# Second expert's weight quarters made during attention, input quarters on VectorE, closer routing rounds, and q and k loaded into unused rows of the accumulator

## The chip, the cores and the metric

One core of one Trainium2 chip. The metric is the device time of one execution in microseconds (us), median of several. All runs used here are of the fast state or, for single looks, of state unknown; one execution of before, of 861.91 us, is marked slow, and no ratio contains it. Two more sources of spread turn out to matter in this case: the clock granted to TensorE (its records show full and half speed: up to the last matmul, 41.0 us of half speed in the first trace of before, 20.5 us in its third), and the end of an execution. From the last matmul to the end, while the last outputs are written, the 16 traces took 13.0 to 17.4 us, with no order by kernel.

## The reference, cut to what matters

```python
# attention: 4 batches x 8 heads, 768 positions of 64; scores only where 6-bit hashes agree
mask = q_bucket[:, :, :, None] == k_bucket[:, :, None, :]
attn = softmax(where(mask, scale * q @ k.T, -1e9)) @ v
x = attn.transpose(0, 2, 1, 3).reshape(3072, 512)
# routing: eight rounds over P [3072, 8]
P = exp(x @ w_gate - max)
for _ in range(8):
    P /= P.sum(1, keepdims=True) + 1e-09
    P /= P.sum(0, keepdims=True) + 1e-09
    P *= N / E
# eight experts over all positions, weighted by P
out += P[:, e:e+1] * (maximum(x @ w1[e], 0) @ w2[e])
```

## The kernel before

Attention runs in eight groups (a batch and four heads each). Group n+1 is prepared while group n is computed: load q and k, transpose on VectorE (DVE), cast on GpSimd (POOL), then 26 small transfers on one queue (SyncE's; for group 0 those of q go on ScalarE's) that bring the data into the layout for the scores. The hash bits make a detour through DRAM: `ds<-kb`, `ks<-ds`.

```python
def prepare(n):
    ...
    hashed("q"); put_bits("q"); stack("q", 1)
    if n == 0:
        fetch(1, "kq")                 # bulk load of the next group, 1.5 MB, GpSimd's queue
    elif n + 1 < len(groups):
        fetch(n + 1, "q")
    ...
    get_bits("q")                      # the last small transfers of group n
    cast_v()
    if n + 1 < len(groups):
        fetch(n + 1, "v")
    if n in (1, 3):
        load_w(0, (n + 1) // 2, pin=True)
```

After attention comes what is called the transition here: the eight routing rounds, between which TensorE (PE) does steps of the first expert for the last batches, counted at 650 ns each:

```python
def plain():
    yield from first_hidden(B - 1)     # 16 steps
    yield from first_combine(B - 2)    # 16 steps
    yield from first_combine(B - 1)    # 16 steps
    yield from first_of(1, 0)          # first product of expert 1, batch 0, alone

quarters_of_x(0); quarters_of_w(1)     # GpSimd
for it in range(ITERS):
    halves = routing(it)
    next(halves)                       # VectorE: row sums, division, column sums
    got = 0
    while got < (5500 if it == 0 else 3900):
        got += next(steps, 99999)      # TensorE
    for _ in halves: pass              # TensorE: cpt = ones x column sums; VectorE: scale
for _ in steps: pass
for b in range(1, B):
    quarters_of_x(b)                   # GpSimd
```

Experts 1 to 7 form their first product with seven products of quarter matrices instead of eight (Strassen's scheme), for which sums and differences of the quarters of the input (`xd`) and of the weights (`s`) are made beforehand, four instructions each time. In those later stages the first product of one batch is woven with the second product of the batch before.

The softmax here doesn't subtract the row's maximum and nothing guards it: scores larger than these inputs give would overflow.

Of the kernel before, what the change touches and what calls it, by code (L numbers as in the profile page):

```python
# [8 lines left out]
F32 = mybir.dt.float32  # L9
# [10 lines left out]
def kernel(  # L20
# [11 lines left out]
    nc = tc.nc  # L32
# [73 lines left out]
    acc = big.tile([P, NBLK, DD], F32)  # L106
    wpool = ctx.enter_context(tc.tile_pool(name="wpool", bufs=2))
    hpool = ctx.enter_context(tc.tile_pool(name="hpool", bufs=2))

    weights = {}  # L110

# [11 lines left out]

    hts = {}
    outv = out.rearrange("(b r j m) d -> b j m r d", b=B, r=R, j=J)

    def combine(e, b):
        if (e, 2) not in weights:
# [37 lines left out]
                yield 650  # L166

    actx = ExitStack()
    ld = actx.enter_context(tc.tile_pool(name="ld", bufs=2))
    lv = actx.enter_context(tc.tile_pool(name="lv", bufs=1))  # L170
    wk = actx.enter_context(tc.tile_pool(name="wk", bufs=2))
    scr = actx.enter_context(tc.tile_pool(name="scr", bufs=4, space=bass.MemoryType.DRAM))
# [7 lines left out]
    def fetch(n, what, eng=nc.gpsimd):  # L180
        b, g = groups[n]
        for name, src in (("k", k), ("q", q)):
            if name in what:
                t = ld.tile([P, M, D], F32, tag="nat", name=name)
                pin(eng.dma_start(out=t, in_=src[b, g * HG:(g + 1) * HG].rearrange("h (r m) d -> (h r) m d", r=R)))
                nat[name, n] = t
        if "v" in what:
            t = lv.tile([P, HG, KT * D], F32, tag="v", name="v")
            vsrc = v[b, g * HG:(g + 1) * HG].rearrange("h (r m j) d -> m r h (j d)", r=R, m=M4)
            for m in range(M4):  # L190
                pin(eng.dma_start(out=t[R * m:R * (m + 1)], in_=vsrc[m]))
            nat["v", n] = t

    def prepare(n):
# [87 lines left out]
        hashed("q")  # L282
        put_bits("q")
        stack("q", 1)
        if n == 0:
            fetch(1, "kq")
        elif n + 1 < len(groups):
            fetch(n + 1, "q")
        yield 6 + 3 * lag
        if n:  # L290
# [1 line left out]
        get_bits("q")  # L292
        cast_v()
        if n + 1 < len(groups):
            fetch(n + 1, "v")
        if n in (1, 3):
            load_w(0, (n + 1) // 2, pin=True)
        if n == 2:
# [105 lines left out]
    for u in range(len(units) + 1):  # L404
        if u < len(units):
            n, h, kt = units[u]
            b, g = groups[n]
            i = u % per
            if i == 0:
                prep = prepare(n + 1) if n + 1 < len(groups) else iter(())  # L410
                due = 0
            while due is not None and due <= i:
                due = next(prep, None)
            if u + 1 < len(units):
                pts[u + 1] = scores(*units[u + 1])
        if u > 0:
            values(*units[u - 1], pts.pop(u - 1))
        if u == len(units):
            break
        if kt == 3 and h % 2 == 0 and u > 5:  # L420
            pn, ph = (n, h - 1) if h else (n - 1, HG - 1)
            pb_, pg = groups[pn]
            turn(pb_, pg * 2 + ph // 2)
            if pg == NGRP - 1 and ph == HG - 1:
                fill = filler(pb_, pb_ < 2)
                owed = 0.0
        elif u >= 2 * per:
            owed += (total if b < 3 else total - 12 * 865) / (2 * per - 8)
            while owed > 0:
                c = next(fill, None)  # L430
                if c is None:
                    break
                owed -= c
                if c == 0:
                    break
        if u % (2 * per) == 2 * per - 1:
            for _ in fill:
                pass
# [36 lines left out]
    xdp = ctx.enter_context(tc.tile_pool(name="xdp", bufs=1))  # L475

    xd = xdp.tile([P, 3, 2, B, HT], F16)
    spool = ctx.enter_context(tc.tile_pool(name="spool", bufs=2))
    upool = ctx.enter_context(tc.tile_pool(name="upool", bufs=2))
    quarters = {}  # L480
    def quarters_of_x(b):
        v = xT[:, :, b * S:(b + 1) * S].rearrange("p (dh d) (th t) -> p dh th d t", dh=2, th=2)
        b11, b12, b21, b22 = v[:, 0, 0], v[:, 0, 1], v[:, 1, 0], v[:, 1, 1]
        t2, t3, t4 = (xd[:, i, :, b, :] for i in range(3))
        eng = nc.gpsimd
        eng.tensor_tensor(t3, b22, b12, op=Alu.subtract)
        eng.tensor_tensor(b12, b12, b11, op=Alu.subtract)
        eng.tensor_tensor(t2, b22, b12, op=Alu.subtract)
        eng.tensor_tensor(t4, b21, t2, op=Alu.subtract)
        quarters[b] = dict(b11=b11, b21=b21, b22=b22, t1=b12, t2=t2, t3=t3, t4=t4)  # L490

    def quarters_of_w(e):

        t = weights[e, 1]
        lo, hi = slice(0, F // 2), slice(F // 2, F)
        a11, a12, a21, a22 = t[:, 0:2, lo], t[:, 2:4, lo], t[:, 0:2, hi], t[:, 2:4, hi]
        s = spool.tile([P, 3, 2, F // 2], F16, tag="s1")
        nc.gpsimd.tensor_tensor(s[:, 0], a21, a22, op=Alu.add)
        nc.gpsimd.tensor_tensor(a21, a11, a21, op=Alu.subtract)
        nc.gpsimd.tensor_tensor(s[:, 1], s[:, 0], a11, op=Alu.subtract)  # L500
        nc.gpsimd.tensor_tensor(s[:, 2], a12, s[:, 1], op=Alu.subtract)
        weights[e, "q"] = dict(a11=a11, a12=a12, a22=a22, s1=s[:, 0], s2=s[:, 1], s3=a21, s4=s[:, 2])

    add = nc.vector._custom_dve

    def hidden(e, b):


        if b == 2 and e < E - 1:
            if (e + 1, 1) not in weights:  # L510
                load_w(e + 1, 1)
            quarters_of_w(e + 1)
        wq, xq = weights[e, "q"], quarters[b]
        hT = hpool.tile([P, FO, S], F16, tag="h")
        hts[e, b] = hT
        lo, hi = slice(0, HT), slice(HT, S)

        def prod(bk, f, wn, xn, first):
            for do in range(2):
                yield nc.tensor.matmul(bk, wq[wn][:, do, f * P:(f + 1) * P], xq[xn][:, do, :],  # L520
                                       start=first and do == 0, stop=do == 1, skip_group_check=True)

        def keep(bk, tag):
            t = upool.tile([P, HT], F32, tag=tag, name="u")
            nc.scalar.copy(t, bk)  # L525
            return t

        def add_relu(dst, bk, u):
            add(TENSOR_ADD_SAT, out=dst, in0=bk, in1=u, s0=3e38, s1=0.0)  # L529

        def last(f, d, u2):
            yield from prod(d, f, "a22", "t4", False)
            add_relu(hT[:, FH + f, lo], d, u2)

        late = iter(())
        for f in range(FH):
            a = hps.tile([P, HT], F32, tag="a", name="a")
            yield from prod(a, f, "a11", "b11", True)
            u1 = keep(a, "u1")
            d1 = dps.tile([P, HT], F32, tag="d", name="d1")  # L540
            yield from prod(d1, f, "a12", "b21", True)
            add_relu(hT[:, f, lo], d1, u1)
            yield None
            yield from prod(a, f, "s2", "t2", False)
            u2 = keep(a, "u2")
            d2 = d2ps.tile([P, HT], F32, tag="d", name="d2")
            yield from prod(d2, f, "s3", "t3", True)
            yield None
            yield from prod(a, f, "s1", "t1", False)
            u3 = keep(a, "u3")  # L550
            add_relu(hT[:, FH + f, hi], d2, u3)
            yield from late
            yield None
            yield from prod(a, f, "s4", "b22", False)
            nc.scalar.activation(out=hT[:, f, hi], in_=a, func=Act.Relu)  # L555
            late = last(f, d2, u2)
            if f == FH - 1:
                yield from late
                late = iter(())
            yield None  # L560
# [15 lines left out]
            else:  # L576
                pin(ins)

    def first_of(e, b):
        for ins in hidden(e, b):  # L580
            if ins is None:
                yield 650
            else:
                pin(ins)

    def plain():
        yield from first_hidden(B - 1)
        yield from first_combine(B - 2)
        yield from first_combine(B - 1)
        yield from first_of(1, 0)  # L590

    quarters_of_x(0)
    quarters_of_w(1)
    steps = plain()
    for it in range(ITERS):
        halves = routing(it)
        next(halves)
        got = 0
        while got < (5500 if it == 0 else 3900):
            got += next(steps, 99999)  # L600
        for _ in halves:
            pass
    for _ in steps:
        pass
    for b in range(1, B):
        quarters_of_x(b)
    work = [(e, b) for e in range(1, E) for b in range(B)]
    for n in range(1, len(work) + 1):
        h = hidden(*work[n]) if n < len(work) else iter(())
        c = combine(*work[n - 1])  # L610
        more = True
        while more:
            more = run(h, True)
            more = run(c, True) or more


# [28 lines left out]
```

## Time and profile before

| | before |
|---|---|
| time, median of 4 | 848.65 us (847.55 to 849.67) |
| the execution that was traced | 858.17 us, span 856.4, mean granted clock 0.969 |
| transition (first L162 matmul to the end of the first one of the second expert's combine) | 66.65 us |
| from there to the last matmul | 547.0 us |
| last matmul to the end | 16.3 us |

The prediction counts the transition to the start of that last matmul and so has 66.4 us. The second row is to be kept in mind. The trace is of an execution 9.5 us slower than the median. I saw this difference and passed over it.

How to read the views: the page's slices give the busy tenths of each engine in forty equal slices. A row of the timeline gives start, duration, engine, line, operation, output and inputs; in brackets stands the idle time before it and what ended it. A row of the waits gives total, number and longest, in us.

### The profile page before, as it was taken

The page shows a single profiled execution, that of the slowest core. Times are in us where ns is not written, and L with a number is a line of the kernel's source. Part 1 is how long each engine was busy: PE and PEld are TensorE (multiplying, and loading weights), DVE is VectorE, ACT ScalarE, POOL GpSimd, SP SyncE. Part 2 cuts the span into 40 slices and gives each one's busy share as a digit, 9 for nine tenths or more (in the row PEclk, how much of TensorE's full clock was granted, in tenths as well). Part 3 has the DMA queues.
Part 4 walks back from the last instruction along what each step waited for, and adds up shares of the span by engine and source line. Part 5 has one row for each costly group of instructions (what it writes and reads, how often), then busy time and mean ns, then how long its engine had stood idle before and what let it go on. Part 6 is the DMA issues. An engine that isn't in the chain of part 4 may idle for free.

```text
span 856.4 us, 13672 instructions
## 1 busy us (share of the span) xinstructions
PE 794.9 (93%) x5404; PEld 429.3 (50%) x5404; DVE 447.5 (52%) x773; ACT 394.9 (46%) x698; POOL 192.0 (22%) x212
## 2 busy tenths in 40 slices
PE   3699999999877899999999999999999999999992
PEld 1466656566533455555555555555555555555540
DVE  4135646554487455555555555555555555555551
ACT  0587766678622555543333333433333333333320
POOL 7555245530496000120040004000400310000000
PEclk9689999999988999999999999999999999999997
DMA  7866678520002300230023003202300230001222
GB/s 226 202 158 151 145 165 201 135 59 17 1 1 49 51 1 1 50 50 1 0 50 50 1 8 54 39 1 49 50 2 1 50 50 1 1 0 59 78 77 82
DMA packets 31927, 50.60 MB, mean 59 GB/s; under 512 B 8504, under 2 KB 21304, under 8 KB 31864
## 3 DMA queue, kind: packets, MB, share of 16 engines
q0 software_dynamic: 16880, 33.30, 19.1%
q1 hardware_dynamic: 14316, 15.95, 6.9%
q8 instruction: 42, 0.69, 0.3%
q10 hardware_dynamic: 668, 0.49, 0.2%
q14 instruction: 21, 0.17, 0.1%
HBM read 53.14 MB, written 7.08 MB: 70 GB/s over the span
## 4 chain that ended last, share of the span: by engine, by line
PE 61%; DVE 4%; issue 0%; ACT 0%; ACTq 0%
PE yp L140 32%; PE a L520 16%; PE d L520 13%; DVE hT L529 3%; ACT u L525 0%; DVE acc L146 0%; ACT hT L555 0%; ACTq L525 0%
## 5 line engine op out<-in xcount | busy, mean ns | idle before, releaser
L140 PE MATMUL yp<-t,hT 128*128 128x512 f16 x1440 | 386.3, 382 | 0.0
L525 ACT COPY u<-a 128x384 f32<-128x384 f32 x336 | 161.1, 480 | 246.3 <-PE a L520 241.3
L529 DVE CUSTOM_DVE_ANT_0 hT<-d,u 128x384 f16<-128x384 f32 x336 | 179.3, 554 | 148.8 <-PE d L520 90.2
L140 PEld LDWEIGHTS <-hT 128*128 128x128 f16 x1440 | 141.8, 99 | 125.8 <-issue 5.3
L146 DVE SCALAR_TENSOR_TENSOR acc<-yp,p,acc 128x512 f32<-128x512 f32 x168 | 125.9, 749 | 114.7 <-PE yp L140 112.2
L310 ACT ACTIVATE pt<-st 128x768 f16<-128x768 f32 x192 | 147.3, 809 | 73.0 <-PE st L307 46.5
L520 PEld LDWEIGHTS <-t 128*128 128x128 f16 x896 | 87.8, 98 | 78.7 <-issue 11.4
L307 PE MATMUL st<-qs,ks 71*128 71x384 f16 x384 | 98.3, 339 | 17.2 <-DMA qs<-ds 13.0
L520 PE MATMUL d<-xd,t 128*128 128x384 f16 x448 | 109.3, 326 | 4.1 <-DVE hT L529 0.3
L520 PE MATMUL a<-xT,s 128*128 128x384 f16 x448 | 109.3, 325 | 2.3 <-ACT u L525 2.3
L520 PEld LDWEIGHTS <-s 128*128 128x128 f16 x672 | 65.8, 98 | 87.1 <-issue 13.4
L555 ACT ACTIVATE hT<-a 128x384 f16<-128x384 f32 x112 | 55.0, 491 | 74.6 <-PE a L520 74.1
L119 POOL DMA_DIRECT2D t<-in_moe_w_dram x16 | 13.5, 846 | 327.3 <-PE d L520 307.4
L323 PEld LDWEIGHTS <-pt 128*128 128x128 f16 x1152 | 62.8, 100 | 28.5 <-issue 3.9
L323 PE MATMUL num<-va,pt 128*128 128x65 f16 x1152 | 68.6, 197 | 0.6 <-ACT pt L310 0.6
L520 PE MATMUL a<-xd,s 128*128 128x384 f16 x224 | 54.7, 326 | 0.9 <-ACT u L525 0.9
L520 PE MATMUL d<-xT,t 128*128 128x384 f16 x224 | 55.1, 328 | 0.0
L520 PE MATMUL a<-xT,t 128*128 128x384 f16 x224 | 55.1, 328 | 0.0
L307 PEld LDWEIGHTS <-ks 71*128 71x128 f16 x384 | 33.4, 100 | 38.3 <-issue 13.0
L217 POOL CAST t<-acc 128x768 f16<-128x768 f32 x32 | 26.3, 827 | 92.1 <-DVE acc L216 60.7
L368 DVE TENSOR_SCALAR hT<-hp 128x384 f16<-128x384 f32 x48 | 26.7, 555 | 28.6 <-PE hp L365 28.6
L365 PE MATMUL hp<-xT,t 128*128 128x384 f16 x192 | 39.0, 325 | 0.0
(75 smaller groups left out, 452.2 us busy)
## 6 DMA issues: line engine op xcount, KB each, us to landing
t<-in_moe_w_dram POOLq DMA_DIRECT2D x16, 1024.0 KB, 8.8
out_dram<-acc SPq DMA_DIRECT2D x24, 256.0 KB
k<-in_k_dram POOLq DMA_DIRECT2D x7, 768.0 KB, 5.7
q<-in_q_dram POOLq DMA_DIRECT2D x7, 768.0 KB, 6.3
v<-in_v_dram POOLq DMA_DIRECT2D x28, 192.0 KB, 4.3
ks<-t SPq DMA_DIRECT2D x64, 48.0 KB
qs<-t SPq DMA_DIRECT2D x56, 48.0 KB
k<-in_k_dram SPq DMA_DIRECT2D x1, 768.0 KB
```

The lines of the kernel that those rows point to most:

```text
L140: yield nc.tensor.matmul(yp, hT[:, fo, j * P:(j + 1) * P], w2[:, fo, :], start=(fo == 0), stop=(fo == FO - 1))
L146: nc.vector.scalar_tensor_tensor(out=acc[:, blk, :], in0=yp, scalar=pw_[-1][:, blk, e:e + 1], in1=acc[:, blk, :], op0=Alu.mult, op1=Alu.add)
L217: pin(nc.gpsimd.tensor_copy(t16s[name][:, c, :], trs[name][:, c, :]))
L307: pin(nc.tensor.matmul(st[:, i, 0:HT], d["k"][0:KR, h, kt * P:(kt + 1) * P], d["q"][0:KR, h, i * HT:(i + 1) * HT], start=True, stop=True))
L310: pin(nc.scalar.activation(out=pt, in_=st[:, :, 0:HT], func=Act.Exp, scale=scale))
L323: pin(nc.tensor.matmul(num[:, j * (D + 1):(j + 1) * (D + 1)], pf[:, j * P:(j + 1) * P], va[:, h, kt, :], start=(kt == 0 and j == 0), stop= ...
L365: pin(nc.tensor.matmul(hp[:, 0:HT], w1[:, do, fo * P:(fo + 1) * P], xT[:, do, b * S + t * HT:b * S + (t + 1) * HT], start=(do == 0), stop= ...
L368: pin(nc.vector.tensor_scalar(hT[:, fo, t * HT:(t + 1) * HT], hp[:, 0:HT], 0.0, None, op0=Alu.max))
L520: yield nc.tensor.matmul(bk, wq[wn][:, do, f * P:(f + 1) * P], xq[xn][:, do, :], start=first and do == 0, stop=do == 1, skip_group_check=True)
L525: nc.scalar.copy(t, bk)
L529: add(TENSOR_ADD_SAT, out=dst, in0=bk, in1=u, s0=3e38, s1=0.0)
L555: nc.scalar.activation(out=hT[:, f, hi], in_=a, func=Act.Relu)
```

## The change

Its intent: keep GpSimd, beside whose instructions VectorE's took up to 2.33 us instead of 0.36, quiet during the routing rounds, then set the rounds closer. The memory for the weight quarters comes from the q and k buffers, which now land in rows of `acc` that are not used yet. The core of the diff:

```diff
+            if n == len(groups) - 1 and i == 2:
+                quarters_of_w(1)                    # last attention group, GpSimd, pinned
...
-    ld = actx.enter_context(tc.tile_pool(name="ld", bufs=2))
-                t = ld.tile([P, M, D], F32, tag="nat", name=name)
+                x = 12 if name == "k" else 15
+                t = acc[:, x:x + 3, :].rearrange("p a d -> p (a d)").rearrange("p (m d) -> p m d", d=D)
...
-        if n == 0:
-            fetch(1, "kq")
-        elif n + 1 < len(groups):
+        if n and n + 1 < len(groups):
             fetch(n + 1, "q")
...
-            fetch(n + 1, "v")
+            fetch(n + 1, "v" if n else "kqv")
...
-        eng = nc.gpsimd                             # quarters_of_x
+        eng = nc.vector
...
-        yield from first_combine(B - 1)
-        yield from first_of(1, 0)
+        yield from woven(0)                         # both of them, interleaved
...
-        while got < (5500 if it == 0 else 3900):
+        while got < (3500 if it == 0 else 3000):
...
+        if n < B:
+            quarters_of_x(n)                        # just ahead of the batch that reads it
```

## The prediction

> **What bounds the kernel now.** I read the page's slices first, then the waits of TensorE, then the order of work on VectorE and GpSimd where the slices dip. The busy tenths of the page (forty slices of 21.4 us) say where there is anything to win:

> ```profile
> PE   3699999999877899999999999999999999999992
> ...
> POOL 7555245530496000120040004000400310000000
> PEclk9689999999988999999999999999999999999997
> ```

> TensorE (PE) is the bound from about 292 us to 840 us: its waits over that stretch come to 0.3 us in all. The end (840 to 856 us) is the last output transfer, which the change doesn't touch. So only two places can give time back: the first three slices (the start), and slices 10 to 14 (214 to 300 us), where attention ends and the routing rounds run. There GpSimd (POOL) is near full exactly where PE dips. TensorE's waits from 226 to 293 us:

> ```profile
> PE cpt L466 <- DVE cs L462: 9.9, 4, 3.8
> PE a L520 <- ACT u L525: 3.2, 11, 0.4
> ```

> The tiny matmul `cpt`, one of each routing round, waits 9.9 us for VectorE (DVE). The timeline of VectorE shows why one round takes so long while GpSimd works and so little when it doesn't. The start is in the first column, the duration in the second:

> ```profile
> 238.72 1.89 DVE L460 TENSOR_TENSOR p<-p,rs 128x192 f32<-128x192 f32 x1
> ...
> 261.98 0.18 DVE L457 TENSOR_SCALAR rs<-rs 128x24 f32<-128x24 f32 x1
> 262.19 0.30 DVE L458 RECIPROCAL rs<-rs 128x24 f32<-128x24 f32 x1
> 262.52 0.36 DVE L460 TENSOR_TENSOR p<-p,rs 128x192 f32<-128x192 f32 x1
> ...
> 265.22 2.33 DVE L471 SCALAR_TENSOR_TENSOR p<-p,cr 128x192 f32<-128x192 f32 x1
> ...
> 267.97 1.59 DVE L457 TENSOR_SCALAR rs<-rs 128x24 f32<-128x24 f32 x1
> ```

> The same L460 takes 1.89 us at 238 us, with GpSimd busy, and 0.36 us at 262 us, in the four microseconds in which GpSimd waits for a weight transfer. Per round VectorE needs 2.65 us from `cpt` (L468) to the end of L462 when it is alone (0.17 + 0.20 + 0.36 + 0.35 + 0.18 + 0.30 + 0.36 + 0.50 plus gaps); with GpSimd busy the rounds took 6.7, 5.9, 5.6, 5.4 and 7.6 us.

> [...] L457, L460 and L471[...] range from 0.18 or 0.36 up to 2.33 us, while the reductions stay at 0.35 and 0.50 us and L468, which reads PSUM, at 0.17 us. [...] half speed from 240.66 for 6.83 us after the wait of 2.70 us, and from 271.38 for 6.83 us after the one of 3.75 us; after waits of 1.83 and 1.63 us it stayed full. [...] In the trace a small `qs` transfer issued at 12.52 us, just after the bulk load of the next k (11.89 us), landed at 17.97 to 18.83 us; one issued at 10.05 us landed at 11.90 to 12.90 us.

> **The change part by part.** The work on TensorE is the same: same matmuls, another order.

> *Transition, before.* From the first L162 matmul (226.4 us) to the first matmul of the second expert's combine (292.8 us) are 66.4 us. The work in it at the rates seen there: 64 L162 matmuls at 0.177 us (24 took 4.24) = 11.3; 96 L140 at about 0.22 = 21.1; 56 L520 at 0.163 = 9.1; eight `cpt` at about 0.3 = 2.4. Sum 43.9, so 22.5 us are lost: the 9.9 us wait, half-clock stretches (3.41 + 6.83 + 6.83 us, half of it lost, some of it overlapping the wait), and 16.2 us for 9.1 us of L520 work that ran alone at the end, where each product waits for ScalarE.

> *Weight quarters of the second expert.* Four GpSimd instructions of 2.12 us = 8.5 us move into the last attention group, where GpSimd stood idle for 33.8 us. VectorE's instructions there read PSUM, so I expect no contention.

> *Input quarters.* Sixteen GpSimd instructions of 1.67 us (26.7 us) become sixteen on VectorE; estimated at 0.56 us as L342, four take 2.3 us with gaps. Batch 0 lies ahead of round one: VectorE starts at 228.1 instead of 226.8 us but needs 1.9 us for its half instead of 4.7, so it is ready near 230, before TensorE has done six L162 steps (about 232). Batch 1 lies after the last round, and costs an estimated 0.8 us with the sums queued behind it. **Batches 2 and 3 cost something:** they queue behind the previous batch's last accumulation (0.75 us) and the third product of the new batch needs the third result: ready about 0.85 + 3 x 0.59 = 2.6 us after the batch begins, while TensorE gets there after 0.33 + 0.33 + 0.65 = 1.3 us. Near 1.4 us each, 2.8 us together.

> *Rounds closer.* Five steps of about 0.69 us between rounds instead of six, so a round is 3.5 us of TensorE work, against 2.65 + 0.5 us of VectorE with hand-over. TensorE, not VectorE, sets the pace, if GpSimd keeps quiet. **It doesn't wholly:** the third expert's weights no longer queue behind the input quarters; their buffer is free when L162 ends (about 239 us), the load takes 8.1 us (257.07 to 265.21 before), so its four instructions run about 248 to 257 us, inside rounds five and six. Some four contended VectorE instructions at about 1.3 us extra each give 4.5 us of waiting, and half a chance of a half-clock stretch of 6.83 us, 1.7 us on average.

> *Weaving.* The 9.1 us of L520 work that took 16.2 us now runs between L140 matmuls, as in the later stages, where nothing waits.

> Sum after: 43.9 + 1.7 (the half-clock stretch at the end of attention stays) + 4.5 + 1.7 + 0.8 = 52.6 us. Gain 66.4 - 52.6 = 13.8, less 2.8 = **11.0 us**.

> *Start.* The first scores wait until 27.1 us for the small transfers that the bulk load of group 1 holds up. The change issues that load after the casts of v, at about 17.2 us. The small transfers issued from 11.8 to 16.5 us then take about 2 us each instead of 4 to 6; the last ones (from 17.8 us) still meet the load. I put the first scores at 22 to 23 us. The next group's preparation starts from k data landing near 23 us; before, its casts began at 25.75 us, for want of a buffer. So most of the shift carries over: **4 us**, between 1 and 6. Landing q and k in rows of the accumulator keeps one place for each, as the two-buffer pool had in effect; no time.

> Together 15.0 us: 848.9 - 15 = **834 us**.

> **The rivals.** *One:* the start gains nothing, since the next group's chain of some 40 small transfers on one queue sets when group 1 can start (the trace has a wait of 0.72 us on a `qs` transfer at 49.4 us), or the later bulk load makes that wait longer. For it: that chain is nearly as long as the group's attention. Against: it also starts earlier. Result 838. *Two:* VectorE becomes the bound of the transition, with quarters, routing and sums in one queue and TensorE waiting on `hT` or on the input quarters. VectorE was 70% busy there (46.5 of 66.4 us), but about half of that was contention that leaves. Result 838 to 842. *Three:* the third expert's quarters miss the rounds or hurt little, no half-clock stretch follows, and the start gives 5 to 6 us: gain 19 to 22, result 827 to 830. *Four:* the transition is hidden anyway. Against it stands the wait of 9.9 us on TensorE itself, with TensorE the bound before and after.

> **Range and chances.** The two large terms are uncertain by about 4 us (contention, clock) and 2.5 us (start), together about 5: 827 to 841. The 2% line is at 831.9 us, a gain of 17 us, two beyond my sum: 33% for faster. Slower needs something unseen: 2%.

> **What would show it.** In the profile after: L457, L460 and L471 at 0.18 and 0.36 us except in one stretch of about 8.5 us where GpSimd makes the third expert's quarters; the wait of `cpt` at 3 to 6 us; the second expert's combine starting about 18 us earlier than at 292.8; the input quarters on VectorE near 0.56 us; TensorE waiting 1 to 1.5 us on `xd` at two later batches; the first score matmul at 22 to 23 us. I am wrong if the first scores hardly move, if f16 subtractions take over 0.8 us, if the rounds wait for VectorE throughout, or if attention itself grows.

## The result, and the profile after

The changed kernel takes **841.35 us** (840.06 to 843.48, 4 runs) against 848.65: ratio 0.9917, interval 0.9891 to 0.9942. A ratio compares the fast runs of two kernels in the same rounds; it is near the ratio of the medians, but not equal to it. That is a gain of 7.3 us where 15 were forecast, and just outside the range of 827 to 841.

The traces, though, differ by 17.6 us: span 856.4 before, 838.8 after. Of these, 3.3 us lie after the last matmul (16.3 and 13.0 us), which the change doesn't touch. The slices of the page after:

```profile
PE   3869999999889999999999999999999999999993
...
POOL 7645245534031000400040004001300310000000
PEclk9879999999999999999999999999999999999997
```

In slices 11 to 13 (counted from 0; about 231 to 294 us) TensorE is fuller, and GpSimd is nearly empty there. TensorE's waits from 220 us to the end:

```profile
PE cpt L481 <- DVE cs L477: 3.5, 2, 3.1
PE a L520 <- DVE xd L502: 3.1, 2, 1.5
```

The wait for the rounds fell from 9.9 to 3.5 us. A new one is there, 3.1 us on the input quarters of batches 2 and 3. VectorE's timeline (L457 and L460 are L472 and L475 now):

```profile
235.66 0.18 DVE L472 TENSOR_SCALAR rs<-rs 128x24 f32<-128x24 f32 x1
235.87 0.30 DVE L473 RECIPROCAL rs<-rs 128x24 f32<-128x24 f32 x1
236.21 0.36 DVE L475 TENSOR_TENSOR p<-p,rs 128x192 f32<-128x192 f32 x1
...
245.97 2.12 DVE L472 TENSOR_SCALAR rs<-rs 128x24 f32<-128x24 f32 x1
248.13 0.30 DVE L473 RECIPROCAL rs<-rs 128x24 f32<-128x24 f32 x1
248.47 2.00 DVE L475 TENSOR_TENSOR p<-p,rs 128x192 f32<-128x192 f32 x1
```

The rounds run at full speed until 245.9 us and are hit once more, until about 254.7 us. GpSimd's timeline says by what:

```profile
190.25 2.12 POOL L136 TENSOR_TENSOR s<-t 128x1024 f16<-128x1024 f16 x1
...
238.14 0.78 POOL L120 DMA_DIRECT2D t<-in_moe_w_dram  x1 [39.30 <-PE cpt L481]
245.94 2.12 POOL L136 TENSOR_TENSOR s<-t 128x1024 f16<-128x1024 f16 x1 [7.02 <-DMA t<-in_moe_w_dram]
```

The second expert's quarters were made at 190 us, inside attention; VectorE's instructions there that read PSUM (L348, L355, L381) took 0.55 to 0.56 us beside them and after them. The third expert's load went out as soon as its buffer came free (238.1), and its four instructions start at 245.9, in the rounds. The input quarters took 0.55 to 0.56 us each on VectorE, as estimated from the copy L342 (768 f16 elements, 0.56 us). So far every step of the prediction is there. The start is another matter. These are TensorE's first scores of group 0 and of group 1, before and then after:

```profile
27.14 1.44 PE L307 MATMUL st<-qs,ks 71*128 71x384 f16 x4 [10.77 <-DMA qs<-ds]
...
49.44 0.77 PE L307 MATMUL st<-qs,ks 71*128 71x384 f16 x2 [0.72 <-DMA qs<-ds]
```

```profile
20.08 1.44 PE L320 MATMUL st<-qs,ks 71*128 71x384 f16 x4 [4.90 <-DMA qs<-ds]
...
48.19 0.80 PE L320 MATMUL st<-qs,ks 71*128 71x384 f16 x2 [7.46 <-DMA ks<-t]
```

Group 0 began at 20.1 us instead of 27.1, earlier than predicted, but group 1 only 1.3 us earlier: the 7 us have become a wait of 7.5 us. (The row names the transfer that landed last before the scores, `ks<-t`, issued at 45.95 us for group 2. Group 1's own last transfers, `qs<-ds`, landed from 46.6 us on.)

### The profile page after: what moved, and what is told of

It is laid out like the page before. It is cut to its first block, busy times and chain, and to the rows that moved or that the text cites. A ratio compares the mean times of both kernels' runs of the same rounds, so it can differ in the third digit from the quotient of the medians.

```text
span 838.8 us, 13662 instructions
## 1 busy us (share of the span) xinstructions
PE 786.6 (94%) x5404; PEld 427.1 (51%) x5404; DVE 440.2 (52%) x789; ACT 394.9 (47%) x698; POOL 165.8 (20%) x196
## 4 chain that ended last, share of the span: by engine, by line
PE 83%; DVE 6%; DMA 5%; ACT 2%; SPq 1%; issue 1%; POOL 1%; ACTq 0%; POOLq 0%; DVEq 0%
PE yp L155 34%; PE a L520 17%; PE d L520 14%; PE st L320 6%; PE hp L378 4%; DVE hT L529 4%; PE num L336 3%; PE yp L388 2%; ACT pt L323 2%; PE hp L177 1%; DMA ks<-t 1%; PE pr L243 1%; DMA v<-in_v_dram 1%; DMA acc<-in_q_dram 1%; DMA ds<-kb 1%
## 5 line engine op out<-in xcount | busy, mean ns | idle before, releaser
L525 ACT COPY u<-a 128x384 f32<-128x384 f32 x336 | 161.1, 480 | 252.8 <-PE a L520 243.7
L520 PEld LDWEIGHTS <-t 128*128 128x128 f16 x896 | 87.8, 98 | 78.7 <-issue 10.8
L520 PE MATMUL d<-xd,t 128*128 128x384 f16 x448 | 109.5, 326 | 3.9
L520 PEld LDWEIGHTS <-s 128*128 128x128 f16 x672 | 65.6, 98 | 87.0 <-issue 8.3
L520 PE MATMUL a<-xT,s 128*128 128x384 f16 x448 | 109.3, 326 | 0.0
L120 POOL DMA_DIRECT2D t<-in_moe_w_dram x16 | 13.5, 846 | 374.0 <-PE d L520 295.2
L520 PE MATMUL a<-xd,s 128*128 128x384 f16 x224 | 55.1, 328 | 3.1 <-DVE xd L502 3.1
L520 PE MATMUL d<-xT,t 128*128 128x384 f16 x224 | 55.1, 328 | 0.0
L520 PE MATMUL a<-xT,t 128*128 128x384 f16 x224 | 55.0, 327 | 0.0
L381 DVE TENSOR_SCALAR hT<-hp 128x384 f16<-128x384 f32 x48 | 26.7, 555 | 28.6 <-PE hp L378 28.6
```

The source lines that it names most:

```text
L381: pin(nc.vector.tensor_scalar(hT[:, fo, t * HT:(t + 1) * HT], hp[:, 0:HT], 0.0, None, op0=Alu.max))
L520: yield nc.tensor.matmul(bk, wq[wn][:, do, f * P:(f + 1) * P], xq[xn][:, do, :], start=first and do == 0, stop=do == 1, skip_group_check=True)
L525: nc.scalar.copy(t, bk)
```

## The experiments

The theory after the first reading (A): the mechanism is as predicted; the time is short of it because the trace of before was a slow execution, with half-clock stretches that the median execution doesn't have, and because the start's gain is lost in a wait. Rival (B): a traced execution is always slower for this kernel, and the change does something in timed executions that no trace shows. Unless noted, a run's numbers are its ratio to before of the same rounds and, from its trace, the transition. Half-clock figures are sums from the trace's clock records up to the last matmul; a stretch can cover a wait (of the 17.07 us from 18.79 us in the first trace, 8.35 lie before the first scores), so they bound a loss and are not one. The transition is counted as in the table above.

**b1 and a1: both kernels again.** No edit.

> The kernel before once more, unchanged, for a second trace. Theory A (the trace that the prediction was worked from was a slow execution: 858.2 us against 847.5 to 849.7 in all others): this trace has a span of 845 to 849 us, with the missing 8 to 10 us in fewer half-clock stretches (before: 34 us of half clock up to the last matmul) and in the end (16.3 us from the last matmul to the end against 12.9 in the trace of after), and its transition is 58 to 63 us instead of 66.4. Rival B (a profiled execution of this kernel is always slower than a timed one): the span is near 856 us again, with the same stretches.

> The changed kernel once more. Theory A: span 838 to 842 us, transition near 50 us (first trace: 225.05 to 275.20), end near 13 us; ratio to before 0.990 to 0.993. Rival B: the same; this run tells how much of a difference between two traces is chance.

Measured: b1's ratio 1.0022 (0.9969 to 1.0075). Its traced execution took 859.72 us, its three others 850.6 to 853.2; transition 66.6 us, half clock 41.0 us. So the expected 845 to 849 us did not come, and rival B was favoured. (The 34 us of half clock that this expectation gives for the first trace are 41.0 by its records.) a1's ratio was 0.9933 (0.9897 to 0.9969), transition 51.0 us. Its traced execution was 5.2 us longer than the first one of the changed kernel (845.69 and 840.54), although its last matmul came only 0.8 us later: the end took 17.3 us instead of 13.0.

**start_only: the later load alone, in before.**

```diff
-        if n == 0:
-            fetch(1, "kq")
-        elif n + 1 < len(groups):
+        if n and n + 1 < len(groups):
             fetch(n + 1, "q")
-            fetch(n + 1, "v")
+            fetch(n + 1, "v" if n else "kqv")
```

> Kernel before with one part of the change: the loads of k and q of group 1 go out with v, after the casts. Theory A: the first scores start near 20 us instead of 27 us, but only 1 to 2 us are left at the end of attention, because group 1 then waits 4 to 6 us for its own qs transfers; time 0.5 to 2 us below before (ratio 0.998 to 0.9995). Rival (the start carries over, as predicted): 4 us less, ratio 0.995.

Measured: ratio 0.9984 (0.993 to 1.0037). First scores at 19.9 us, group 1 at 47.6 us after a wait of 6.8 us, transition (which this edit leaves alone) 62.4 us. **after_early_fetch** is the reverse edit in the changed kernel.

> The changed kernel with the loads of k and q of group 1 back in their old place. Theory A: first scores near 27 us again; the attention ends 1 to 2 us later than in the changed kernel, time 842 to 843 us, ratio to before 0.992 to 0.995. Rival (the start carries over): 845 us.

Measured: ratio 0.9937 (0.9889 to 0.9985), beside 0.9933 for the changed kernel in the same rounds; first scores at 26.2, group 1 at 49.7 us. By these ratios the start is worth about 1 us, but their intervals are wide: 0.993 would be 6 us, more than the 4 predicted. The traces decide. Attention ended (the first matmul of the transition) at 224.5 to 228.2 us in the six traces with the early load, on average 226.3, and at 224.4 to 227.8 us in the eight with the late load, on average 225.3. (Left out are w1_late and best_warm, which change attention further.) That is 1.0 us, and not 4.

**ports_only and order_only: the two halves of the transition.** The first is the changed kernel with the old thresholds and the old, unwoven `plain`; the second is before with the new ones:

```diff
-        yield from first_combine(B - 1)
-        yield from first_of(1, 0)
+        yield from woven(0)
-        while got < (5500 if it == 0 else 3900):
+        while got < (3500 if it == 0 else 3000):
```

> The changed kernel with the old order on TensorE: nine and six steps between the rounds instead of six and five, the third batch's combine and the second expert's first product not woven. Quarters and start stay as in the change. Theory A (keeping GpSimd quiet is what shortens the transition; closer rounds and weaving add some 5 us): L472, L475, L486 at 0.18 to 0.36 us outside the third expert's quarters, wait of cpt under 4 us, transition 54 to 57 us (after: 50.4 and 51.0, before: 66.6), time 3 to 5 us above the changed kernel. Rival (the order alone does it): transition above 60 us, time as before.

> Kernel before with the new order on TensorE alone: closer rounds and weaving, all quarters on GpSimd as before. Theory A: VectorE's contended instructions stay at 1 to 2.3 us, a round takes 5.5 to 7 us against 3.4 us of TensorE work, so the wait of cpt grows from 9.9 to 14 to 20 us; weaving gives back about 6 us, transition 62 to 67 us, time within 4 us of before. Rival (order alone does it): transition under 57 us.

Measured: ports_only 0.9948 (0.9927 to 0.9969), transition 54.2 us; order_only 1.0006 (0.9983 to 1.0028), transition 61.6 us. TensorE's waits in the transition, ports_only and then order_only:

```profile
PE a L520 <- ACT u L525: 3.6, 12, 0.4
PE cpt L481 <- DVE cs L477: 2.3, 1, 2.3
```

```profile
PE cpt L466 <- DVE cs L462: 11.8, 6, 3.1
```

Closer rounds and weaving alone gain nothing: what weaving removes (the wait on ScalarE) the rounds give back, as they still wait for VectorE. My figure of 14 to 20 us for that wait was too high. Once GpSimd is quiet, the order shortens the transition by 3.2 to 3.8 us in the traces (54.2 against 50.4 to 51.0). I expected 3 to 5 us of it in the times; ports_only's ratio and those of the changed kernel (0.9917 and 0.9933) are too close to show it.

**quiet: the third expert's quarters after the rounds.** One tiny GpSimd copy in front of them reads the last input quarter of batch 1:

```diff
+        if e == 2:
+            pin(nc.gpsimd.tensor_copy(mark16, quarters[1]["t4"][:, 0, 0:1]))
         s = spool.tile([P, 3, 2, F // 2], F16, tag="s1")
```

> The changed kernel, with the third expert's weight quarters held back by one tiny copy that reads the last quarter of batch 1, so that they run after the rounds. Theory A (the 3.5 us wait of cpt left in after, and the half-clock stretch behind it, come from GpSimd's four instructions): wait of cpt under 0.8 us, L472 and L475 at 0.18 and 0.36 us in all rounds, no half-clock stretch between 232 us and the last matmul, transition 45 to 47 us, time 3 to 5 us below the changed kernel. Rival (VectorE's own queue, sums and quarters, makes the wait): no change.

Measured: 836.32 us, ratio **0.9811** (0.9786 to 0.9836), transition 46.4 us. Its wait of cpt, and GpSimd's timeline:

```profile
PE cpt L485 <- DVE cs L481: 0.4, 1, 0.4
```

```profile
259.65 0.18 POOL L138 COPY mark<-xd 128x1 f16<-128x1 f16 x1 [19.95 <-DVE xd L506]
259.79 2.12 POOL L140 TENSOR_TENSOR s<-t 128x1024 f16<-128x1024 f16 x1
```

So the remaining wait of cpt was GpSimd's doing. The transition is 4 to 4.6 us shorter in the traces; the ratio fell by more (0.9917 and 0.9933 to 0.9811). Its timed executions had a mean clock of 0.977 to 0.984, those of the changed kernel 0.973 to 0.981; part of the surplus may be clock, part may be the end (13.5 us in its trace; 13.0, 17.3 and 16.4 in the three of the changed kernel). The timed executions leave no trace to show which.

**w1_late: the first expert's 1 MB weight load one group later.**

```diff
-        if n in (1, 3):
-            load_w(0, (n + 1) // 2, pin=True)
+        if n in (2, 3):
+            load_w(0, n - 1, pin=True)
```

> The changed kernel with the first expert's 1 MB weight load one group later. Theory A (the start's gain is lost because group 1's last small transfers stand behind that load: qs transfers issued at 42.5 to 45.1 us landed at 46.6 to 48.3, with the load landing at 45.7 to 47.4): group 1 starts at 44 to 46 us instead of 48.2, and 1 to 3 us of it are left at the end of attention. Rival (the queue that issues the small transfers is the limit): group 1 starts at 47.5 to 48.5 us, no gain.

```profile
44.78 0.80 PE L320 MATMUL st<-qs,ks 71*128 71x384 f16 x2 [2.87 <-DMA qs<-ds]
```

Measured: group 1 starts at 44.8 us, as theory A had it, so the load was what held up its small transfers (in the eight traces with the load in place and the late fetch, group 1 started at 47.6 to 50.2 us). Yet the ratio is 0.9932 (0.9907 to 0.9957), the same as the changed kernel's. In the trace a wait of 3.8 us on the same kind of transfer stands at the start of group 2, now with the load in front of them, a half-clock stretch of 13.7 us follows, and group 3 starts at 101.9 us instead of 96.3. Attention ended at 230.5 us, where 1 to 3 us of gain were expected. The wait had moved on by one group. This trace is of the slowest of the six executions (849.39 us; the others took 843.5 to 847.0), so the 5.6 us are not typical.

**b2 and a2: third traces.** No edit, a single look each (state unknown).

> Kernel before, a third trace. Two traces had 40.9 and 41.0 us of half clock up to the last matmul and spans of 856.4 and 857.9 us, while timed executions of before took 847.6 to 856.7 us at a mean clock of 0.971 to 0.979 (0.969 and 0.970 in the two traces). Theory A (where a wait falls in the clock's windows is chance): half clock of 27 to 34 us, transition 60 to 64 us, time 849 to 853 us. Rival B (the traced execution is always slow): again 41 us, 66.5 us, 857 us.

> The changed kernel, a third trace. The two so far had 23.9 us of half clock up to the last matmul; its timed executions had a mean clock as low as 0.973, that is about 44 us over the span. Theory A: 24 to 37 us, the stretch behind the cpt wait 3.4 or 6.8 us long, transition 50 to 53 us. Rival B: 23.9 us again.

a2: 846.87 us, transition 50.6 us, half clock 30.7 us. b2: 847.33 us, span 845.5 us, transition **59.2 us**, half clock 20.5 us, all three below what I expected. Its mean clock of 0.982 is above that of each of the 40 timed executions below, so it shows what is possible and not what is typical. The transition of before in its first trace and in b2, as stretches (columns: length; busy time and, in brackets, instructions of PE, weight loads, DVE, ACT, POOL; granted clock; DMA share; GB/s):

```profile
226.40:293.05 66.65, 53.17 (x244) 25.38 (x241) 46.65 (x76) 22.77 (x46) 44.02 (x26) 0.87 0.20 32
```

```profile
225.20:284.40 59.20, 47.73 (x242) 23.26 (x240) 44.06 (x76) 22.67 (x46) 44.24 (x26) 0.97 0.22 36
```

The same instructions but for a few records, the same GpSimd time, and 5.4 us less TensorE busy time: the clock. Most of the other 2 us are shorter waits of cpt (8.0 us instead of 9.9). TensorE's timeline around the second round, in the first trace and in b2:

```profile
241.19 0.59 PE L466 MATMUL cpt<-cs,ones 128*128 128x8 f32 x2 [2.70 <-DVE cs L462]
...
242.87 5.68 PE L140 MATMUL yp<-t,hT 128*128 128x512 f16 x15
```

```profile
239.94 0.39 PE L466 MATMUL cpt<-cs,ones 128*128 128x8 f32 x2 [2.71 <-DVE cs L462]
...
240.84 3.40 PE L140 MATMUL yp<-t,hT 128*128 128x512 f16 x15
```

Over the 40 timed executions of before in the rounds of these experiments, time goes with the mean granted clock (correlation -0.87, and -0.85 without the slow one): the five at 0.970 or less took 857.6 to 861.9 us, the other 35 took 847.8 to 856.7. The trace that I predicted from (858.2 us at 0.969) is like the five. The mean clock is a blunt measure, though: it counts the end as well, most of it idle and at half clock (11.6 of the last 16.3 us in the first trace), so a long end lowers the clock and lengthens the time without costing any work.

**early_x and quiet_early_x: input quarters ahead of need.** In both, the four instructions for batches 2 and 3 go one at a time into the stage before; the second also has the edit of quiet.

```diff
+        ahead = quarters_of_x(n + 1) if n + 1 < B else iter(())
-        for _ in woven(n):
-            pass
+        for i, _ in enumerate(woven(n)):
+            if i % 4 == 1 and i >= 5:
+                next(ahead, None)
```

> The changed kernel, with the input quarters of batches 2 and 3 made one instruction at a time inside the stage before. Theory A (TensorE's two waits of 1.5 us on xd, 3.1 us together, are the queue position and not VectorE's load): these waits vanish, the stretch from the second expert's first combine to the last matmul is 547 to 547.5 us (after: 550.4 and 550.5; before: 547.0), time 3 us below the changed kernel. Rival (VectorE is full there): waits on hT of the same size appear instead.

> Both mends in the changed kernel: third expert's quarters after the rounds, input quarters ahead of need. Theory A: wait of cpt under 0.8 us, no wait on xd, transition 46 to 47 us, later stretch 547 us, ratio to before 0.976 to 0.980, so faster by over 2%. Rival (the GpSimd instructions now collide with the input quarters on VectorE): the quarters of batch 2 take over 1 us each, waits on hT appear, ratio 0.981 or more.

Measured: early_x 839.59 us, ratio 0.9846 (0.9797 to 0.9896), a wider gain than the 3 us expected, with a wide interval; no wait on `xd`, no new one on `hT`, and the stretch from the second expert's first combine to the last matmul is 547.0 us, as in before, where the changed kernel has 550.4 to 550.5. The queue position it was. quiet_early_x: **835.02 us** (832.44 to 836.23), ratio **0.9792** (0.9749 to 0.9836), transition 45.5 us, later stretch 547.0 us. It beats before, and by their ratios the changed kernel too; whether it is over 2% faster than before the interval leaves open. The mean of before was raised in these rounds by two executions of 857.6 and 859.1 us (the slow one is left out); by medians (851.81) it is 2.0%.

**before_warm and best_warm: is it the waits that trip the clock?** The first is before with idle-filling matmuls ahead of the second round's cpt; the second is quiet_early_x with 28 of 512 columns ahead of group 1's first scores.

```diff
+        if it == 1:
+            busy = d2ps.tile([P, HT], F32, tag="d", name="busy")
+            for _ in range(15):
+                pin(nc.tensor.matmul(busy, ident, xT[:, 0, 0:HT], start=True, stop=True))
```

> Kernel before with 15 idle-filling matmuls (about 2.4 us, results unused) in front of the second round's cpt, where three traces show a wait of 2.7 us. Theory A (that wait trips the clock in most executions, and the stretch costs 3 us and more): no half-clock stretch between 232 and 262 us, transition 58 to 61 us, ratio to before 0.993 to 0.998. Rival (the stretches are not caused by this wait): a stretch of 6.8 us near 240 us remains in the trace, transition above 63 us, ratio 1.000 or more.

> quiet_early_x with 28 idle-filling matmuls (about 6 us at full clock) in front of the first scores of group 1, where TensorE waits 7.2 us for small transfers. Theory A: the half-clock stretch of 10.2 us near 44 us goes or shrinks to 3.4 us, group 1 takes 20 to 21 us instead of 22.3, time 1 to 2.5 us below quiet_early_x, ratio to before 0.974 to 0.979. Rival (group 1 is set by the exponentials and the next group's transfers, whatever the clock): group 2 still starts near 70 us, ratio as quiet_early_x.

before_warm: transition 59.9 us and full clock through the rounds in its trace (a half-clock stretch of 3.41 us at 274.2 us comes after the last round's cpt, at 273.32). Here are the stretches from 232 us, first trace of before, then before_warm (columns as above):

```profile
232.00:282.00 50.00, 39.09 (x173) 18.31 (x172) 37.17 (x62) 14.76 (x29) 38.42 (x23) 0.86 0.19 30
```

```profile
232.00:272.00 40.00, 34.81 (x179) 16.91 (x177) 31.86 (x56) 13.74 (x27) 35.83 (x21) 1.00 0.16 27
```

So filling that wait brings the transition that b2 had by luck. But the ratio is 0.9986 (0.9948 to 1.0025), above the 0.993 to 0.998 expected: the average timed execution had at most 4.4 us to save there (if the filling costs nothing itself), so not all of them can have lost the 6.7 us by which the first trace is longer. How many had a stretch stays open; of four traces of that transition with the wait left in (the first, b1, start_only, b2) three had one behind it, of 6.83, 6.83 and 3.41 us. best_warm: ratio 0.9796 (0.9759 to 0.9834), as quiet_early_x. The stretch near 44 us went, another of 10.2 us came at 71 us, and group 1 started at 49.4 instead of 47.9 us, group 3 at 99.7 instead of 96.3. No gain.

## Why the prediction was wrong, point by point

- **What bounds, and GpSimd slowing VectorE: right.** L457, L460 and L471 fell to 0.18 and 0.36 us wherever GpSimd was quiet. The lost time stands in the durations, with no idle time before them, and mostly on one side: in the first trace L471 took up to 2.33 us instead of 0.36, while GpSimd's instructions of 2.12 us took 2.24 at most. ports_only and order_only show that this is what pays and that the order alone doesn't.
- **The third expert's quarters in the rounds: right.** Predicted at 248 to 257 us with 4.5 us of waiting; measured from 245.9 us, 3.5 us (4.2 in the traces of a1 and a2). quiet confirmed the cause.
- **Transition after: nearly right.** Predicted 52.6 us, measured 50.4, 51.0 and 50.6.
- **Batches 2 and 3: right.** Predicted 2.8 us, measured 3.1 us of waits and 3.4 us on the later stretch (550.4 against 547.0); early_x took it away.
- **The start: mis-sized, "4 us, between 1 and 6".** The first scores came even earlier (20.1 us), but in the changed kernel group 1 waited 7.5 us. The step that failed is "most of the shift carries over". I had named the rival, but for the wrong reason in part: not the length of the chain (of 26 transfers a group, not 40), but the 1 MB weight load in front of its last transfers. They were issued at 42.5 to 45.1 us and landed at 46.6 to 48.5; the load, issued at 37.3 us in the changed kernel and at 37.5 in before, landed at 45.7 to 47.4 and at 46.6 to 48.1, so it ended at nearly the same time in both. w1_late showed the cause, by one trace, and no gain from moving it. Measured worth: about 1 us. (The transfers of group 0 that I gave 4 to 6 us took 4.4 to 7.0: one of 48 KB, issued at 13.32 us, after the bulk loads of 11.89 and 12.62, had landed by 20.35. Four of the five issued from 10.05 to 11.84 us had landed after 1.9 to 2.9 us, the fifth after 4.6.)
- **The transition before: the main miss.** The step that failed was "From the first L162 matmul to the first matmul of the second expert's combine are 66.4 us ... so 22.5 us are lost", and with it subtracting a gain read from one trace from the median of other executions. Of the three half-clock stretches that I counted there, two (13.7 us) came behind waits of 2.70 and 3.75 us; behind the wait of 2.71 us in b2 there was none. The same transition took 66.6 us in b1, 62.4 in start_only, 59.2 in b2, and 59.9 in before_warm, where the trip at the second round was prevented.

The sum again with the measured terms: a transition of 59.2 to 62.4 (b2 and start_only, whose executions of 847.3 and 849.5 us are near the medians) less 50.6, that is 8.6 to 11.8; less 3.4; plus about 1 for the start: 6.2 to 9.4 us. Measured were 7.3 us in the first rounds and 5.0 us in a1's (medians 851.17 and 846.15). The same sum with my 66.4 gives 13.4, close to the 14.2 us by which the last matmul came earlier in the first pair of traces (840.0 and 825.9). So the working described the pair of traces well, and the pair of medians badly. That the 66.4 us contain clock losses which other executions lack is shown by traces. That the median execution has a transition near 60 us is inferred: timed executions show only their mean clock, and how often they have these stretches, and how long their end is, stays open.

## What to carry to other kernels

Before you work out a gain from a trace, compare that execution's time and granted clock with those of the timed ones. Where the trace is slower, find the stretches of reduced clock in it and count their loss separately, as something that the median may not have; and compare the time after the last matmul, which the change may not touch. An engine with idle time is not free while its instructions lengthen those of the engine on the critical path (2.12 us instead of 0.18 here): an order change that did nothing alone shortened the transition by 3.2 to 3.8 us in the traces once the other engine was quiet. And follow a gain at the start to the next place where something waits; here 7 us became a wait of 7.5 us.
